# An FFT convolution with an expert layer on one core: whole-row loads, loads queued in another order, and an earlier hand-over to the experts

## The chip, the cores and the metric

The kernel runs on one core of a Trainium2 chip. TensorE (PE), VectorE (DVE), ScalarE (ACT) and GpSimd (POOL) compute; SyncE (SP) issues most DMAs, GpSimd issues the indirect ones. Each engine works through its own list of instructions in order. The metric is the time of one execution in microseconds (us), lower is better. The kernel before takes 2277.13 us, the median of three runs (2272.99, 2277.13 and 2289.8 us).

## The reference

```python
def _attn_ref(x, v, pos_emb, w1, w2):          # x, v: (4, 11456, 128)
    h_mlp = np.maximum(pos_emb @ w1, 0.0) @ w2
    h_filt = h_mlp * np.exp(-0.01 * pos)[:, None]
    u = x * v
    Uf = np.fft.rfft(u, n=2 * S, axis=1)
    Hf = np.fft.rfft(h_filt, n=2 * S, axis=0)
    y = np.fft.irfft(Uf * Hf[None], n=2 * S, axis=1)[:, :S, :]
    return x * y

def _moe_ref(x, modality_id, w_gate, modality_bias, w1, w2):   # x: (45824, 128), 8 experts
    logits = x @ w_gate + modality_bias[modality_id]
    e_idx = np.argmax(logits, axis=1)                          # one expert for each row
    gate_w = softmax(logits)[np.arange(N), e_idx]
    for e in range(E):
        mask = e_idx == e
        out[mask] = gate_w[mask, None] * (np.maximum(x[mask] @ w1[e], 0.0) @ w2[e])
```

Four sequences of 11,456 rows are convolved with one long filter; each resulting row then goes to one of eight experts (128 to 1024 to 128).

## The kernel before

**Stages.** Everything is written out in Python loops; a small class, `Timeline`, sorts the pieces by a time step, a place within the step and a rank, and so sets the order in which each engine's instructions are written. The filter comes first. Then, for each sequence b, an outer stage of 16 steps and a middle stage of 23 groups alternate. The outer stage of b does two things at once: it transforms sequence b forward, and it transforms sequence b-1 back and chooses the experts of its rows. So outer stage 0 has forward work alone, outer stages 1 to 3 have both, and a last outer stage (4) has the back half alone. The middle stage works on spectra. Then come the experts: tiles of 512 rows of one expert each, eight steps a tile (`experts`, L961), 99 tiles in all.

**One step of an outer stage.** The table `OUTER` (L57) gives each kind of work its delay in steps: `turn0:0` means that step t does this for q = t, `half:2` that it does it for q = t-2. In DVE's order a step holds: `product` (x times v, then a sum and a difference, L457 to L461), `choice` in every other step (the expert of each row, L758 to L779), `inverse` (L686 to L688, which ends in the multiplication with x into the buffer `xo`) and `send` in every other step (L804 to L811, the rows' places). In PE's order: turns (L672), `half` (L729, transposes of `xo`), `forward` (L472, reads what `product` wrote), `inverse` (L681), `logits`. The kinds in `LATE` (load, load_x, store, places) come at the end of a step; their DMAs are all in SP's one queue.

**The loads.** `load` (L446) brings x and v of block q as a tile of 128 partitions by 4 KB each into a ring of six buffers, three blocks deep. The sequences fill partitions 0 to 44 and 64 to 108; the rest of such a tile is padding. The first three blocks of a stage are read whole, to fill the buffers; later ones in two DMAs of 45 rows. `load_x` (the `load` at L662) brings another layout of x for `inverse` into a ring of four that it shares with the results y. The load of block q overwrites buffers of block q-3, which `forward` of q-3 reads on PE.

**Rows to the experts.** `store` (L784) writes rows of `xo` (three buffers) with their weight and number to DRAM (`xr`), `places` (L813) their target places (`xi`). When a sequence is done, `fetch` reads the places, and `rows_back` (L243) reads the rows, five blocks of 128 at a time, into one of three buffers; `send_rows` (L255) scatters one block of 128 rows per indirect DMA (L263) to its expert's region of `xs`. There are 90 blocks for each sequence. They are handed out in small numbers behind DVE instructions of the next stages (`paced`), at most eight under way at a time. `rows_back` for the next five is called with the first block of the present five, and waits until the buffer's former five are scattered.

**The hand-over.** A table of expert tiles (`first_table`) is computed from the counts known so far: `first` = 60 tiles that are surely full after three of four sequences. DVE computes it during the last outer stage. The load of a tile's rows (`rows_in`, L977) waits for the scatters that its table rests on. The last block of choices of sequence 3 (choice and store, then send and places) is left to the expert steps 8 and 14 (`FA`, `FB`), and its 90 scatters to later ones, with a second and a third table (`rest`).

Of the kernel before, what the change touches and what calls it, by code (L numbers as in the profile page):

```python
# [12 lines left out]
F32 = mybir.dt.float32  # L13
# [34 lines left out]
def surely_full(n):  # L48
# [7 lines left out]
NOWHERE = 1 << 20  # L56
OUTER = ("turn0:0 turn1:0 lturn:3 biased:3 half:2 product:-1 forward:1 choice:3 "  # L57
         "inverse:0 logits:2 send:4 load:-2 load_x:-2 store:4 places:5")
LAST = ("inverse:1 logits:3 turn0:0 half:2 lturn:3 turn1:0 biased:4 choice:4 load_x:-1 store:4 "
# [8 lines left out]
UNSURE = 5  # L68
FA, FB, FC = 8, 14, 18
NDYN = 8  # L70
# [106 lines left out]
def hyena_moe_kernel(ctx: ExitStack, tc: tile.TileContext, a: dict, out: bass.AP,  # L177
# [77 lines left out]
    def send_rows(n, behind=None, wait=None):  # L255


        for _ in range(min(n, len(waiting))):
            b, c = waiting.pop(0)
            if c % RC == 0:  # L260
                rows_back(b, c // RC + 1)
            ix, src = to_t[b % 2][:, c:c + 1], back_t[(b * NB + c // RC) % 3][:, c % RC]
            s = pool.indirect_dma_start(  # L263
                out=xs, out_offset=bass.IndirectOffsetOnAxis(ap=ix, axis=0), in_=src,
                in_offset=None, bounds_check=E * R - 1, oob_is_err=False)
            free_rows(scatters, s)
            if behind is not None:
                tc.add_manual_dep(ins_of(s), behind.name, order_dep, reason="order of issue")
            if wait is not None:
                tc.add_manual_dep(ins_of(s), wait.name, sync_dep, reason="pace")  # L270


    first = surely_full((nb - 1) * S) if nb > 1 else 0
    NW1 = min(nt, first)
# [79 lines left out]
    with ExitStack() as cv:  # L354
# [88 lines left out]
        def forward_stages(b):  # L443
            kept = {}

            def load(q):  # L446
                if q == 0:
                    from_first("seq")
                for name in ("xd", "v"):
                    t = kept[q, name] = ring("seq")  # L450
                    for p in (slice(0, HALF), slice(64, PU)) if q > 2 else (slice(0, D),):
                        sp.dma_start(t[p], a[name][b, q, p])

            def product(q):

                u, e = kept.pop((q, "xd"))[0:PU], kept.pop((q, "v"))[0:PU]
                paced(dve.tensor_mul(u, u, e))  # L457
                e = kept[q, "e"] = e.rearrange("p (c m) -> p c m", c=2)
                u = u.rearrange("p (w m) -> p w m", w=2)
                dve.tensor_add(e[:, 0], u[:, 0], u[:, 1])  # L460
                paced(dve.tensor_sub(e[:, 1], u[:, 0], u[:, 1]))  # L461

            def transform(q):

                e = kept.pop((q, "e")).rearrange("p c (j n) -> p c j n", n=N2)
                for h in range(2):
                    p = pair("s1")
                    for j in range(4):
                        for c in range(2):
                            for blk in range(2):  # L470
                                at = slice(64 * blk, 64 * blk + HALF)
                                pe.matmul(p[64 * c:64 * c + 64, blk, N1 * j:N1 * j + N1],  # L472
                                          e[at, c, 4 * h + j], fwd[at, c], start=True, stop=True)
# [351 lines left out]

        def before_last(f):
            return lambda q: f(q) if q < NQ - 1 else None

        def outer(b, at):
# [15 lines left out]
            if b == nb:  # L845
                for name in ("choice", "send", "store", "places"):
                    todo[name] = before_last(todo[name])
                finale.extend([lambda: (choice(NO - 1), store(NO - 1)),
                               lambda: (send(NO - 1), places(NO - 1))])
            def when(name, i, d):  # L850
# [24 lines left out]
        for b in range(nb + 1):  # L875
            outer(b, at)
            if b < nb:
# [5 lines left out]
                for k in range(3):  # L883
                    line.put(at - 1, lambda k=k: bias_of(k), 4, k)
            if b == nb - 1:
                line.put(at - 3, lambda: (dve.tensor_copy(base1, base),
                                          known.append((nb - 1) * NR // D)), 3)
        if NW1:
            gen = first_table(place)
            line.put(at - 1, lambda: [next(gen, 0) for _ in range(6)], 2)  # L890
            for k in range(NQ + 3):
                line.put(at + k, lambda: next(gen, 0), 3)
            line.put(at + NQ + 3, lambda: [0 for _ in gen], 4)
        else:
# [3 lines left out]
        line.run()  # L898
        send_rows(len(waiting))

# [13 lines left out]
    def rest():  # L914


        sp.dma_start(pad, a["c_pad"].rearrange("p (j r) -> p j r", j=TH // D))
        sp.dma_start(xs[E * R:E * R + TH, :].rearrange("(p j) r -> p j r", j=TH // D), pad)
# [42 lines left out]
    def experts(lo, hi):  # L961
# [116 lines left out]
        def rows_out(i):  # L1078
# [5 lines left out]
            for j in range(n // D):  # L1084
                pe.transpose(pt[:, D * j:D * j + D], k["oT"][:, D * j:D * j + D], ident)
            ot = mt.tile([D, 4, D], F32, tag="ot", name="ot", bufs=8)
            dve.tensor_mul(ot[:, 0:n // D], pt[:, 0:n].rearrange("p (j d) -> p j d", d=D),  # L1087
# [12 lines left out]
        for at in range(len(work) + 6):  # L1100
# [4 lines left out]
            if at < 2:  # L1105
                weights(lo, 2 + at)
            if lo == 0 and at in (FA, FB):
                finale[at == FB]()
            if lo == 0 and at == FC:
                fetch(nb - 1)  # L1110
            if lo == 0 and 4 * at % 15 < 4:
                send_rows(1)
            if NW1 - 14 <= i < NW1:
                next(others, 0)
# [57 lines left out]
```

## Time and profile before

| | |
|---|---|
| median of three runs | 2277.13 us |
| profiled execution | 2273.27 us |
| its span, first to last instruction | 2271.3 us |
| mean granted TensorE clock in it | 0.959 |
| PE busy | 2083.2 us (92%) |
| DVE busy | 1774.8 us (78%) |
| ACT busy | 1324.6 us (58%) |
| POOL busy | 1025.3 us (45%) |
| bytes moved by DMA | 343.10 MB |

The profile is of one execution. A busy share over the whole span mixes stages that are limited by different things, so it has to be cut into stages first: the filter up to about 100 us, outer stages from about 100, 283, 536, 795 and 1049 us on, middle stages from 172, 430, 688 and 949 us on, the experts from 1175 us to 2256 us. PE's clock in the rows is the granted share of full speed; 0.50 is the lower of its two levels.

### The profile page before, as it was taken

How to read it: one execution, taken by the hardware profiler on the slowest of the kernel's cores; microseconds unless marked ns; L12 is line 12 of the kernel's file. 1: busy time of each engine (PE TensorE's matmuls, PEld its weight loads, DVE VectorE, ACT ScalarE, POOL GpSimd, SP SyncE). 2: the span in 40 equal slices, each digit the busy share in tenths (PEclk: the TensorE clock that was granted, in tenths of full speed). 3: DMA queues.
4: the chain of work that ended last, by engine and by line, in shares of the span. 5: the costliest groups of instructions: out<-in, count | busy, mean ns of one | idle time of the engine just before them, and what ended most of it. 6: DMA issues, size and time to landing. Idle time of an engine off the chain costs nothing. (4 is left out here: it accounts for less than half of the span.)

```text
span 2271.3 us, 47560 instructions
## 1 busy us (share of the span) xinstructions
PE 2083.2 (92%) x17370; PEld 1633.9 (72%) x17370; DVE 1774.8 (78%) x2790; ACT 1324.6 (58%) x2467; POOL 1025.3 (45%) x932
## 2 busy tenths in 40 slices
PE   9979899788887888889969999999999999999996
PEld 8866656565555655566548888888888888888896
DVE  2368988998769977898767777777777877777796
ACT  5644466445544465445546666666666666666675
POOL 0104400396546955487735545555543333333332
PEclk9959999999889989999979999999999999999998
DMA  3886667677877778785768322222212111111110
GB/s 117 325 209 223 227 182 205 220 264 249 236 222 246 258 224 246 216 283 176 214 191 270 117 64 65 78 70 70 70 52 71 48 46 45 42 47 48 36 42 29
DMA packets 191990, 343.10 MB, mean 151 GB/s; under 512 B 33825, under 2 KB 101517, under 8 KB 191753
## 3 DMA queue, kind: packets, MB, share of 16 engines
q1 hardware_dynamic: 165097, 280.63, 40.6%
q0 software_dynamic: 26496, 59.36, 7.6%
q8 instruction: 139, 2.28, 0.4%
q14 instruction: 98, 0.80, 0.1%
q10 hardware_dynamic: 160, 0.03, 0.0%
HBM read 255.48 MB, written 84.83 MB: 150 GB/s over the span
## 5 line engine op out<-in xcount | busy, mean ns | idle before, releaser
L1054 DVE SCALAR_TENSOR_TENSOR hl<-ph,hh 128x512 fp32r<-128x512 f32 x724 | 498.8, 689 | 227.1 <-ACT hh L1053 217.6
L1053 ACT ACTIVATE hh<-ph 128x512 fp32r<-128x512 f32 x724 | 434.2, 600 | 361.7 <-PE ph L1050 357.3
L1090 POOL DMA_INDIRECT out<-ot,idx x362 | 357.3, 987 | 617.8 <-DVE ot L1087 511.6
L263 POOL DMA_INDIRECT xs<-back,to x360 | 433.0, 1203 | 210.5 <-issue 71.4
L1048 PE MATMUL ph<-xh,wh 128*128 128x512 f32 (+1 forms) x792 | 304.0, 384 | 2.0 <-ACT wh L1019 2.0
L1071 PE MATMUL po<-hh,wh 128*128 128x512 f32 (+1 forms) x792 | 303.4, 383 | 0.0
L1073 PE MATMUL po<-hl,wh 128*128 128x512 f32 (+1 forms) x792 | 295.3, 373 | 0.0
L1050 PE MATMUL ph<-xl,wh 128*128 128x512 f32 (+1 forms) x792 | 295.2, 373 | 0.0
L1049 PE MATMUL ph<-xh,wl 128*128 128x512 f32 (+1 forms) x792 | 294.1, 371 | 0.0
L1072 PE MATMUL po<-hh,wl 128*128 128x512 f32 (+1 forms) x792 | 294.0, 371 | 0.0
L649 PE MATMUL pw<-work 64*128 64x128 f32 x2880 | 205.8, 284 | 38.4 <-POOL work L637 31.2
L649 PEld LDWEIGHTS pw<-work 64*128 64x128 f32 x2880 | 174.1, 187 | 86.9 <-POOL work L637 44.8
L653 ACT COPY A<-pw 128x512 f32<-128x512 f32 (+1 forms) x184 | 97.1, 580 | 210.7 <-PE pw L649 210.7
L624 POOL TENSOR_TENSOR work<-work 128x512 f32<-128x512 f32 (+1 forms) x92 | 115.7, 1258 | 217.1 <-DVE work L620 211.8
L630 DVE TENSOR_TENSOR work<-pz,work 128x2048 f32<-128x2048 f32 (+1 forms) x92 | 205.5, 2234 | 0.0
L614 PE MATMUL pz<-A,work 128*64 128x256 f32 x1440 | 182.7, 397 | 16.6 <-DMA work<-in_c_to 7.9
L1050 PEld LDWEIGHTS ph<-xl,wh 128*128 128x128 f32 x792 | 149.4, 189 | 27.1
L1073 PEld LDWEIGHTS po<-hl,wh 128*128 128x128 f32 x792 | 149.1, 188 | 27.2 <-DVE hl L1054 0.2
L1048 PEld LDWEIGHTS ph<-xh,wh 128*128 128x128 f32 x792 | 149.6, 189 | 25.7 <-ACT wh L1019 2.4
L1049 PEld LDWEIGHTS ph<-xh,wl 128*128 128x128 f32 x792 | 150.0, 189 | 24.4 <-DVE wl L1020 0.4
L1072 PEld LDWEIGHTS po<-hh,wl 128*128 128x128 f32 x792 | 149.6, 189 | 22.9
L1071 PEld LDWEIGHTS po<-hh,wh 128*128 128x128 f32 x792 | 149.3, 189 | 22.2
(172 smaller groups left out, 3644.2 us busy)
## 6 DMA issues: line engine op xcount, KB each, us to landing
work<-hs SPq DMA_DIRECT2D x88, 512.0 KB
work<-in_x SPq DMA_DIRECT2D x64, 512.0 KB
work<-in_c_to SPq DMA_DIRECT2D x111, 256.0 KB
xr<-xo SPq DMA_DIRECT2D x64, 365.6 KB
back<-xr SPq DMA_DIRECT2D x72, 325.0 KB
work<-in_c_back SPq DMA_DIRECT2D x88, 256.0 KB
x<-xs SPq DMA_DIRECT2D x82, 260.0 KB
work<-in_xd SPq DMA_DIRECT2D x104, 180.0 KB
```

The costliest lines, as they stand in the source:

```text
L263: s = pool.indirect_dma_start(out=xs, out_offset=bass.IndirectOffsetOnAxis(ap=ix, axis=0), in_=src, in_offset=None, bounds_check=E * R - 1 ...
L630: dve.tensor_mul(m0[:, 0:n * 8 * D].rearrange("p (t c b d) -> p t c b d", c=2, b=2, d=D), z.unsqueeze(2).broadcast_to([D, 2 * n, 2, 2, D]) ...
L649: pe.matmul(v[s][:, t, blk], k["p"][at, t, r, blk], k["c"][at, t, r], start=r == 0, stop=r == 1)
L1048: pe.matmul(p, k[0, "h"][:, f:f + D], k["xh"], start=True, stop=False)
L1049: pe.matmul(p, k[0, "l"][:, f:f + D], k["xh"], start=False, stop=False)
L1050: pe.matmul(p, k[0, "h"][:, f:f + D], k["xl"], start=False, stop=True)
L1053: act.activation(hh, ph, AF.Relu)
L1054: dve.scalar_tensor_tensor(hl, ph, 0.0, hh.bitcast(F32), op0=ALU.max, op1=ALU.subtract)
L1071: pe.matmul(po, k[1, "h"][:, f], hh[:, t], start=g == 0, stop=False)
L1072: pe.matmul(po, k[1, "l"][:, f], hh[:, t], start=False, stop=False)
L1073: pe.matmul(po, k[1, "h"][:, f], hl[:, t], start=False, stop=g == NCH - 1)
L1090: s = pool.indirect_dma_start(out=out, out_offset=bass.IndirectOffsetOnAxis(ap=k["idx"][:, j:j + 1], axis=0), in_=ot[:, j, :], in_offset=N ...
```

## The change

Six things are done. The loads of x and v read all 128 partitions of a tile in one DMA in every block, and the product and forward transform use all of them. In `OUTER`, `product` is done one step later (0 in place of -1), `load_x` is issued one step later (-1 in place of -2) and stands ahead of `load` in the step. `rows_back` is called with the third block of five in place of the first. The first table of tiles rests on two sequences in place of three (37 tiles in place of 60) and is computed in fewer, fuller steps. The last two blocks of stores, sends and places, not the last one alone, are left to expert steps (2, 5, 8, 13 and 16). The scatters of sequence 3 come in five of nine expert steps in place of four of fifteen, and what was flushed ahead of the experts is not. One buffer of `ot` goes, of eight.

```diff
-OUTER = ("turn0:0 turn1:0 lturn:3 biased:3 half:2 product:-1 forward:1 choice:3 "
-         "inverse:0 logits:2 send:4 load:-2 load_x:-2 store:4 places:5")
+OUTER = ("turn0:0 turn1:0 lturn:3 biased:3 half:2 product:0 forward:1 choice:3 "
+         "inverse:0 logits:2 send:4 load_x:-1 load:-2 store:4 places:5")
...
-FA, FB, FC = 8, 14, 18
+FINALE, FC = (2, 5, 8, 13, 16), 18
+FR = 9
...
-            if c % RC == 0:
+            if c % RC == 2:
                 rows_back(b, c // RC + 1)
...
-    first = surely_full((nb - 1) * S) if nb > 1 else 0
+    NK = max(nb - 2, 0)
+    first = surely_full(NK * S) if NK else 0
...
-                    for p in (slice(0, HALF), slice(64, PU)) if q > 2 else (slice(0, D),):
-                        sp.dma_start(t[p], a[name][b, q, p])
+                    sp.dma_start(t, a[name][b, q])
...
-                u, e = kept.pop((q, "xd"))[0:PU], kept.pop((q, "v"))[0:PU]
+                u, e = kept.pop((q, "xd")), kept.pop((q, "v"))
...
-                                at = slice(64 * blk, 64 * blk + HALF)
+                                at = slice(64 * blk, 64 * blk + 64)
...
-                for name in ("choice", "send", "store", "places"):
-                    todo[name] = before_last(todo[name])
-                finale.extend([lambda: (choice(NO - 1), store(NO - 1)),
-                               lambda: (send(NO - 1), places(NO - 1))])
+                todo["choice"] = but_last(todo["choice"], 1)
+                for name in ("send", "store", "places"):
+                    todo[name] = but_last(todo[name], 2)
+                finale.extend([lambda: (store(NO - 2), send(NO - 2)), lambda: places(NO - 2),
+                               lambda: choice(NO - 1), lambda: (store(NO - 1), send(NO - 1)),
+                               lambda: places(NO - 1)])
...
-            if b == nb - 1:
+            if b == NK:
                 line.put(at - 3, lambda: (dve.tensor_copy(base1, base),
-                                          known.append((nb - 1) * NR // D)), 3)
+                                          known.append(NK * NR // D)), 3)
...
-        send_rows(len(waiting))
...
-            ot = mt.tile([D, 4, D], F32, tag="ot", name="ot", bufs=8)
+            ot = mt.tile([D, 4, D], F32, tag="ot", name="ot", bufs=7)
...
-            if lo == 0 and at in (FA, FB):
-                finale[at == FB]()
+            if lo == 0 and at in FINALE:
+                finale[FINALE.index(at)]()
...
-            if lo == 0 and 4 * at % 15 < 4:
+            if lo == 0 and 5 * at % 9 < 5:
                 send_rows(1)
-            if NW1 - 14 <= i < NW1:
+            if NW1 - FR <= i < NW1:
                 next(others, 0)
```

Two pieces of the order of instructions follow. Lines of the changed kernel are numbered up to three higher (L452 is L453, L666 is L667, L977 is L980).

SP's queue in outer stage 2, two steps of it, before (`in_xd` and `in_v` are x and v of `load`, `in_x` is `load_x`, `back<-xr` is `rows_back`, `xr<-xo` is `store`, `xi<-ix` is `places`):

```order
L247 DMA back_91<-xr_58 128x650
L452 DMA work<-in_xd 45x1024 x2
L452 DMA work<-in_v 45x1024 x2
L666 DMA work<-in_x 128x1024
L817 DMA xi_63<-ix_87 90x1x8 x2
L247 DMA back_92<-xr_58 128x650
L452 DMA work<-in_xd 45x1024 x2
L452 DMA work<-in_v 45x1024 x2
L666 DMA work<-in_x 128x1024
L788 DMA xr_59<-xo_83 90x1x1040 x2
```

and in the changed kernel:

```order
L248 DMA back_90<-xr_58 128x650
L667 DMA work<-in_x 128x1024
L453 DMA work<-in_xd 128x1024
L453 DMA work<-in_v 128x1024
L818 DMA xi_63<-ix_87 90x1x8 x2
L248 DMA back_91<-xr_58 128x650
L667 DMA work<-in_x 128x1024
L453 DMA work<-in_xd 128x1024
L453 DMA work<-in_v 128x1024
L789 DMA xr_59<-xo_83 90x1x1040 x2
```

`in_x` now stands ahead of the loads of x and v and of the stores, and belongs to the step after; `in_xd` and `in_v` are one DMA each. Beside the same DMAs DVE's `product` is one step later: the instructions of a step keep their places, and the block that is multiplied there is the one before.

The end of SP's queue ahead of the first expert tile, before (`x<-xs` is `rows_in`, `TENSOR_LOAD` and `ISA` read its address):

```order
L788 DMA xr_61<-xo_84 90x1x1040 x2
L666 DMA work<-in_x 128x1024
L817 DMA xi_65<-ix_86 90x1x8 x2
L788 DMA xr_61<-xo_85 90x1x1040 x2
L817 DMA xi_65<-ix_87 90x1x8 x2
L788 DMA xr_61<-xo_83 90x1x1040 x2
L817 DMA xi_65<-ix_86 90x1x8 x2
L974 TENSOR_LOAD tab_98
L977 ISA
L977 DMA x<-xs 128x520
```

and in the changed kernel:

```order
L789 DMA xr_61<-xo_84 90x1x1040 x2
L667 DMA work<-in_x 128x1024
L818 DMA xi_65<-ix_86 90x1x8 x2
L789 DMA xr_61<-xo_85 90x1x1040 x2
L818 DMA xi_65<-ix_87 90x1x8 x2
L977 TENSOR_LOAD tab_98
L980 ISA
L980 DMA x<-xs 128x520
```

The store and the places of the last block but one have left the queue ahead of the first tile's rows; they stand behind the loads of the third tile and of its weights. On PE the three small matmuls of that block's `send` have likewise moved from ahead of the first expert matmul to behind the third step's.

## Rows read from the trace of the kernel before

**Rows 1.** The page's second part: the span in 40 equal slices of 56.8 us, busy share in tenths; PEclk is the granted clock in tenths.

```profile
PE   9979899788887888889969999999999999999996
PEclk9959999999889989999979999999999999999998
```

**Rows 2.** Busy time of each engine (us, with the number of instructions) by stage: start and end of the stretch, its length, PE, PE's weight loads, DVE, ACT, POOL, then granted clock, busy share of the DMA engines, GB/s. In order: the middle of outer stage 0 (eleven steps); middle stage 0; the last outer stage; the gap ahead of the experts; the first expert tiles, and the rest of them.

```profile
121.60:163.20 41.60, 33.33 (x672) 28.33 (x676) 27.70 (x34) 15.17 (x20) 0.00 (x0) 0.53 0.95 208
172.00:283.00 111.00, 97.38 (x1080) 73.08 (x1080) 105.32 (x73) 50.97 (x93) 54.66 (x44) 0.97 0.66 222
...
1049.00:1148.00 99.00, 91.70 (x615) 59.58 (x615) 69.00 (x159) 59.80 (x122) 71.24 (x67) 1.00 0.67 206
1148.00:1175.00 27.00, 9.74 (x51) 5.82 (x43) 13.60 (x44) 5.20 (x12) 8.37 (x7) 0.62 0.53 142
1175.00:1260.00 85.00, 84.04 (x388) 68.64 (x389) 68.21 (x124) 54.67 (x101) 32.35 (x32) 0.98 0.83 264
1260.00:2256.00 996.00, 993.71 (x5088) 840.07 (x5086) 781.25 (x1359) 658.69 (x1216) 414.48 (x420) 1.00 0.18 56
```

**Rows 3.** The same view for stretches of whole pairs of steps, from one `inverse` on DVE (L686) to another: eight steps of outer stage 1, of 2 and of 3, then four early steps of the last outer stage and six late ones.

```profile
317.60:384.30 66.70, 59.74 (x828) 39.22 (x828) 56.97 (x118) 42.85 (x81) 0.00 (x0) 0.95 0.68 197
582.70:660.20 77.50, 64.09 (x840) 41.75 (x840) 56.86 (x117) 44.20 (x83) 41.19 (x36) 0.91 0.87 241
848.90:924.70 75.80, 64.74 (x836) 42.41 (x835) 56.85 (x117) 43.94 (x82) 41.51 (x36) 0.89 0.86 246
1066.50:1089.40 22.90, 22.90 (x158) 15.18 (x157) 15.15 (x34) 15.62 (x31) 17.68 (x18) 1.00 0.57 186
1104.70:1143.20 38.50, 34.51 (x227) 22.08 (x227) 28.70 (x76) 21.65 (x46) 30.27 (x28) 1.00 0.73 215
```

**Rows 4.** The waits of DVE (who waited, for what: us in total, times, longest), asked stage by stage: `product` for the load of v in 285 to 425 us, 545 to 685 us and 805 to 945 us, and `inverse` for the store of `xo` in 1052 to 1150 us.

```profile
DVE work L457 <- DMA work<-in_v: 9.6, 7, 2.6
DVE work L457 <- DMA work<-in_v: 22.1, 10, 4.3
DVE work L457 <- DMA work<-in_v: 20.9, 9, 3.7
DVE xo L688 <- DMA xr<-xo: 12.2, 4, 4.0
```

**Rows 5.** The waits of SP's queue, the same columns: `load_x` behind `inverse` in 545 to 685 us, then `rows_back` behind the scatters in 545 to 685 us and in 1052 to 1150 us.

```profile
SPq L666 <- DVE xo L688: 15.3, 6, 3.8
SPq L247 <- DMA xs<-back,to: 11.6, 8, 2.7
SPq L247 <- DMA xs<-back,to: 58.4, 20, 9.9
```

**Rows 6.** One step of outer stage 2 in order of time (start us, length us, engine, line, what; in brackets how long the engine had been idle and for what): from SP's queue a load of v, from DVE the end of a step (`inverse`) and the `product` that uses the load.

```profile
600.93 0.80 SPq L452 DMA_DIRECT2D work<-in_v  x2
603.14 1.23 DVE L688 TENSOR_TENSOR xo<-work 128x1024 f32<-128x1024 f32 x1
608.64 1.23 DVE L457 TENSOR_TENSOR work<-work 109x1024 f32<-109x1024 f32 x1 [4.27 <-DMA work<-in_v]
```

**Rows 7.** What DMA moved in 84 to 104 us: the summary line, and the transfers issued there, among them the first whole loads.

```profile
DMA packets 2329, 7.25 MB, mean 363 GB/s; under 512 B 255, under 2 KB 255, under 8 KB 2325
...
hs<-work POOLq DMA_DIRECT2D x6, 512.0 KB
...
work<-in_xd SPq DMA_DIRECT2D x3, 512.0 KB
work<-in_v SPq DMA_DIRECT2D x3, 512.0 KB
```

**Rows 8.** The hand-over in order of time, engine by engine (columns as in rows 6): DVE's late `inverse`; PE's last transposes of the choice and its first of the experts; SP's last stores and places and the first loads of expert rows.

```profile
1150.12 1.23 DVE L688 TENSOR_TENSOR xo<-work 128x1024 f32<-128x1024 f32 x1 [5.49 <-DMA xr<-xo]
1162.18 0.69 PE L744 MATMUL lt<-ident,work 128*109 128x128 f32 x4 [0.61 <-ACT work L739]
1171.81 1.09 PE L1031 MATMUL px<-ident,x 128*128 128x128 f32 x4 [8.81 <-DMA x<-xs]
1158.72 2.03 SPq L817 DMA_DIRECT2D xi<-ix  x2
1164.39 3.20 SPq L817 DMA_DIRECT2D xi<-ix  x2
1169.00 0.37 SPq L977 DMA_DIRECT2D x<-xs  x1
```

**Rows 9.** Groups of instructions by line (count, then busy us and mean ns of one, then idle time ahead): in 285 to 425 us DVE's multiplications over 128 and over 109 partitions; in the whole span PE's weight loads of 45 rows by 64 and of 128 rows by 64.

```profile
L688 DVE TENSOR_TENSOR xo<-work 128x1024 f32<-128x1024 f32 x16 | 19.6, 1227 | 0.5
L457 DVE TENSOR_TENSOR work<-work 109x1024 f32<-109x1024 f32 x15 | 18.3, 1221 | 9.6 <-DMA work<-in_v 9.6
...
L472 PEld LDWEIGHTS s<-fwd,work 45*64 45x64 f32 x4096 | 108.2, 158 | 51.3 <-ACT A L475 22.9 <-issue 11.1 <-DVE work L687 6.7
...
L614 PEld LDWEIGHTS pz<-A,work 128*64 128x64 f32 x1440 | 105.4, 141 | 65.8 <-issue 17.1 <-PE pw L649 9.1 <-PE pz L614 1.3
```

**Rows 10.** POOL in the expert steps in order of time (columns as in rows 6): the first scatters of two successive tiles' results (L1090), and one scatter of rows to the experts (L263) with the next.

```profile
1301.43 0.98 POOL L1090 DMA_INDIRECT out<-ot,idx  x1 [4.44 <-DVE ot L1087]
...
1306.56 0.98 POOL L263 DMA_INDIRECT xs<-back,to  x1 [0.31 <-issue]
1307.85 0.98 POOL L263 DMA_INDIRECT xs<-back,to  x1 [0.30 <-issue]
1313.24 0.98 POOL L1090 DMA_INDIRECT out<-ot,idx  x1 [4.41 <-DVE ot L1087]
```

More of the change, by code (lines that the diff above doesn't have):

```diff
@@ L824, in every_other, with but_last @@
             return lambda q: f(q // 2) if q % 2 == 1 else None
-        def before_last(f):
-            return lambda q: f(q) if q < NQ - 1 else None
+        def but_last(f, n):
+            return lambda q: f(q) if q < NQ - 2 * n else None
         def outer(b, at):
@@ L890, in hyena_moe_kernel @@
             line.put(at - 1, lambda: [next(gen, 0) for _ in range(6)], 2)
-            for k in range(NQ + 3):
-                line.put(at + k, lambda: next(gen, 0), 3)
-            line.put(at + NQ + 3, lambda: [0 for _ in gen], 4)
+            for k in range(NQ - 4):
+                line.put(at + k, lambda: (next(gen, 0), next(gen, 0)), 3)
+            line.put(at + NQ - 4, lambda: [0 for _ in gen], 4)
         else:
@@ L914, in rest @@
     def rest():
+        assert not waiting
         sp.dma_start(pad, a["c_pad"].rearrange("p (j r) -> p j r", j=TH // D))
```

## The prediction

> **What bounds the kernel now.** I read the slices first [rows 1]: PE is nearly full from the 23rd slice on and ragged before, so the experts are PE's and the outer and middle stages are not. Then the stages [rows 2]: in the experts PE is busy 993.71 of 996 us at full clock, so nothing done by another engine there can bring time, and nothing costs any that stays hidden. Middle stage 0 has DVE busy 105.32 of 111 us; the change leaves its work alone, and the later middle stages have the same. What is left are the outer stages and the gap of 27 us ahead of the experts, in which PE is busy for 9.74 us at a clock of 0.62.
>
> Within the outer stages I cut out eight equal steps each [rows 3]. Stages 1, 2 and 3 do the same DVE work there, 57 us, and take 66.7, 77.5 and 75.8 us: 8.34, 9.69 and 9.48 us a step. No engine is full: PE has 59.7 to 64.7 us (more at the lower clock), DVE 57. What differs is the DMA share, 0.68 against 0.87 and 0.86, since stages 2 and 3 also scatter a sequence. The waits [rows 4] say who pays: `product` waits for v 22.1 and 20.9 us in stages 2 and 3 and 9.6 us in stage 1. One step shows how [rows 6]: v is issued at 600.93, after the step's forward transform has freed its buffer, and `product` runs at 608.64 after 4.27 us of idling. The load takes some 7 us to land and gets one step of lead, whatever its size. A DVE that idles there is late with `inverse`, which follows, and so frees PE's result banks and the buffer of `load_x` late.
>
> **Product one step later.** DVE's work is the same; the load gets about one step more, 8 to 9 us, against waits of at most 4.3 us [rows 4], so I let this wait go. The forward transform follows `product` by one step in place of two; it comes after a `choice` and an `inverse` on DVE, so I price its wait at nothing; if DVE lags PE by a whole step the same 1 to 3 us a step come back there (second rival). `load_x` ahead of the loads no longer holds the stores behind `inverse` (15.3 us in stage 2 [rows 5]); it has a step less, but its buffer is free long before, so SP issues it without waiting.
>
> How much of the waits is time? From below: nothing, if PE or DMA takes the wait over. From above: PE's own pace, 5.73 us a step in the early last stage, where PE is busy for all 22.90 us [rows 3], plus the forward transform; 7.47 us of PE work a step in stage 1 is the nearest row for both, so at most 2.2 and 2.0 us a step in stages 2 and 3 and 0.9 in stage 1. I take 8.0 us a step for stage 1 and 8.6 for stages 2 and 3: a little over the present stage 1, which still has 9.6 us of the wait and no scatters. That is 0.34, 1.09 and 0.88 us a step. With 12 of 16 steps in the steady state: **-4, -13 and -11 us**, of which I take 2 off stage 2 for the state of its start: -4, -11, -11. Ends: 0 to -10, 0 to -26, 0 to -24.
>
> **Whole rows.** Each step's two loads grow from 4 x 184 KB = 737 KB to 2 x 524 KB = 1049 KB, and from four DMAs to two. The halved form alone moves 208 GB/s at a DMA share of 0.95, or 219 GB/s of busy time [rows 2]; whole rows move 222 at 0.66 (336) in middle stage 0, 264 at 0.83 (318) in the first experts [rows 2], and 363 GB/s where the first whole loads run [rows 7]. So a step's loads take 3.37 us of DMA before and 2.9 to 3.3 after: more bytes, no more time. The Trainium skill, page "DMA: Bandwidth & Descriptors", section "Anatomy of one DMA — SWDGE (gpsimd) path", speaks against it: a fixed time and then the bytes at 436 GB/s, which would add an estimated 0.7 us a step and turn the next term into +9. Its page "SBUF — State Buffer", section "Door 1: The DMA port swizzle", sides with the rows: a copy into the first 64 partitions reaches half the ports, 196 against 328 GB/s at 1 MiB, an estimated 3.8 us before and 3.2 after. The 208 GB/s agree with the second.
>
> Outer stage 0 is where this shows alone: 41.6 us for eleven steps, 3.78 us each, DMA full, PE busy for 3.03 us a step at a clock of 0.53 [rows 2]. With 2.9 to 3.3 us of DMA and PE's 3.03 I expect 3.3 to 3.4 us, 0.4 less in 13 steps: **-5 us**. Ends: +19 (first slower rival) and -10 (PE at full clock). The product over 128 partitions takes no longer (1227 against 1221 ns), nor does a weight load of 64 or more rows (141 for 128 rows, 158 for 45) [rows 9].
>
> **Last outer stage.** It moves no x and v of `load`. Early steps take 5.73 us with PE full, late ones 6.42 us [rows 3]; `inverse` waits 12.2 us for stores of `xo` [rows 4], and once more 5.49 us at the end [rows 8]. The stores are late because SP stands 58.4 us, 20 times 2.9 us, behind scatters for `rows_back` [rows 5]. Asked for two blocks later, two more scatters of about 1.3 us [rows 10] are done, so most of these 2.9 us go, and in stages 2 and 3 the 11.6 us. POOL itself gets no faster. PE idles 7.3 us of the 99 [rows 2] and some 5 us behind it; I take half: **-6 us**, ends 0 and -12.
>
> **Hand-over.** PE's last work of the stage starts at 1162.18 and its first transpose of expert rows at 1171.81, after 8.81 us of idling for the rows. Their load is issued at 1169.00, behind the stores and places of the last block but one, and serves PE 2.81 us later [rows 8]. With these moved behind it, it follows the places of 1158.72, which end at 1160.75; with the same 1.41 us from the last places' end (1167.59) to the issue it goes out at 1162.2, PE starts at 1165.0, 6.8 us earlier: **-7 us**. Ends: 0 (the tile's buffer or table holds it) and -9 (the clock, 0.62 there, falls less). The wait for three sequences' scatters goes too, but cost nothing visible.
>
> **Moved into the experts at no price.** The five pieces are DVE work in stretches where DVE is busy 781 of 996 us and PE was not held by the one block that is already there [rows 2]. Without that cover they would cost the 4 to 5 us of one `choice` and `send`. Scatters: 4.4 in place of 2.1 per tile beside four of results. At 1.29 us each [rows 10] that is 10.9 us of POOL per tile of 11.8 (1301.43 to 1313.24): close to full, but the buffers of `ot`, seven now, hold it, and 90 of them end after some 20 tiles, before the second table's work starts. Tile count and order within an expert's region stay.
>
> **Sum.** -5 -4 -11 -11 -6 -7 = -44 us. The profiled execution took 2273.27 us; that gives 2229, and the median lies 3.9 us above it, so **2233 us**. The scatter of the runs (2273 to 2290) means that 1%, 22.8 us, is about the least that can be told from no change: below 2254.4 is faster, above 2299.9 slower.
>
> **Rivals.**
> - *More than that* (0.08): the steps come down to PE's 7.5 us, and the clock, 0.89 to 0.95 [rows 3], recovers as PE idles less. For it: stage 1 has PE at 90% already. Against: DMA in stage 2 is busy 0.87 of 9.69, 8.43 us a step; with 2.9 to 3.3 us in place of 3.37 that is 8.0 to 8.4, so 8.6 leaves little. -5 -10 -26 -24 -10 -8 = -83 gives 2194.
> - *The wait changes hands* (0.20): PE waits for its banks or `forward` for `product`, and a third of the gain of stages 1 to 3 stays. For it: PE is busy 83 to 90% there [rows 3]. -5 -1 -4 -4 -6 -7 = -27 gives 2250.
> - *The wait for v stays* (0.10): the change does not do what it says, because the load still waits for `forward` three blocks back and DMA holds it for two steps. For it: the DMA share of 0.87. Against: 4.3 us is the longest wait. Only -5 -6 -7 are left: 2259.
> - *Bytes decide, slower* (0.08): whole rows move no faster per byte than halved ones. At 219 GB/s a step's loads take 4.79 us in place of 3.37. Stage 0 is then bound at (3.59 + 1.42) / 0.95 = 5.3 us a step, +19. In stages 2 and 3 DMA work grows from 8.43 and 8.15 us a step to 9.85 and 9.57; at a share of 0.97 that takes 10.15 and 9.87 us: +6 and +5. With -13 from the rest, 2273 + 4 + 17 = 2294. It decides below 247 GB/s, where the loads take 4.25 us and DMA fills 97% of 9.6 us; the rows for whole tiles have 318 or more. The rule of the page "DMA: Bandwidth & Descriptors" in the Trainium skill, bytes alone, is its milder form.
>
> **How the numbers follow.** The forecast has 0.54 and holds 2214 to 2252. Faster: 0.54, 0.08 and 0.14 of the second rival, 0.76. Slower, with 2294 so near the bound: half of the last rival, 0.04. The rest, 0.20, is no change. The range from 2197 to 2266 takes in the forecast, the second and third rivals and the near part of the first.
>
> **What would show it.** `product`'s wait for v near nothing in stages 2 and 3, and their steps at 8.6 us; if the steps stay at 9.5 with that wait gone, look for the new wait on PE or `forward`. The middle of stage 0 at over 250 GB/s and under 3.6 us a step; if not, whole rows are no faster. SP's wait for scatters in the last stage under 20 us. The idle time before the experts' first transpose near 2 us. A PE still full in the experts to the end: if it waits there around the 35th tile, the second table came late, and if results wait for POOL, the denser scatters are to blame; either would make the prediction wrong from a side that I price at nothing.

## The result and the profile after

| | before | after |
|---|---|---|
| median | 2278.23 us (4 runs, 2272.99 to 2289.8) | 2201.3 us (4 runs, 2199.77 to 2203.26) |
| ratio, 95% interval | | 0.9656 (0.9618 to 0.9694) |
| span of the profiled execution | 2271.3 us | 2198.8 us |
| mean granted TensorE clock | 0.959 | 0.984 |
| bytes moved by DMA | 343.10 MB | 359.27 MB |

The change is 77 us faster; 44 were forecast. Medians are of all executions, ratios of the fast ones, without those over 1.5% above the fastest of the same kernel. 16 MB more are moved, and the time is shorter. The slices of the page, as in [rows 1], now of 55 us each:

```profile
PE   8968899898988898889799999999999999999996
PEclk9999999999999999999899999999999999999998
```

The holes in the clock of before are gone, but for the 20th slice, and PE is even from the 21st slice on; before it was so from the 22nd (the prediction read the 23rd). Where the 72.5 us of the spans come from shows when both traces are cut at the same instructions: `inverse` on DVE (first and last of each outer stage) and the first transpose of the experts on PE.

| | before, us | after, us | difference |
|---|---|---|---|
| start to first `inverse` of outer stage 1 | 290.3 | 283.2 | -7.1 |
| outer stage 1, first to last `inverse` | 116.2 | 104.7 | -11.5 |
| outer stage 2 | 131.4 | 107.4 | -24.0 |
| outer stage 3 | 130.3 | 105.1 | -25.1 |
| the three middle stages between | 389.0 | 386.8 | -2.2 |
| last outer stage | 97.6 | 99.0 | +1.4 |
| last `inverse` to first transpose | 17.05 | 10.7 | -6.4 |
| first transpose to the end | 1099.5 | 1101.9 | +2.4 |

The same stretches by busy time (columns as in [rows 2, 3]): the middle of outer stage 0 between the same times as before; eight steps of outer stages 1, 2 and 3; the last outer stage.

```profile
121.60:163.20 41.60, 25.73 (x824) 21.51 (x816) 30.56 (x37) 18.69 (x26) 0.00 (x0) 0.92 0.93 330
```

```profile
324.27:382.84 58.57, 55.94 (x832) 38.39 (x830) 56.24 (x118) 42.64 (x81) 0.00 (x0) 1.00 0.77 264
560.30:619.04 58.74, 55.98 (x832) 38.42 (x830) 56.41 (x119) 42.93 (x81) 42.12 (x36) 1.00 0.98 345
795.78:854.80 59.02, 56.31 (x835) 38.74 (x833) 56.52 (x119) 43.05 (x82) 42.59 (x36) 1.00 0.99 346
988.00:1087.00 99.00, 88.65 (x570) 57.72 (x568) 66.01 (x158) 56.99 (x117) 76.48 (x72) 0.95 0.64 197
```

The three stages take 7.32, 7.34 and 7.38 us a step, whether a sequence is scattered beside them or not. DVE is busy for 56.2 to 56.5 us of each 58.6 to 59.0, 96%: its own work, 57 us before too [rows 3], is nearly what a step now lasts. PE follows at 95%, with 56 us in place of 59.7 to 64.7, all at a clock of 1.00; which of the two would hold a step alone was not tried. DMA is at 0.98 and 0.99 in stages 2 and 3, at 345 GB/s where it moved 241 and 246.

DVE's waits in outer stages 1, 2 and 3 (283 to 388, 517 to 625 and 754 to 860 us), the heads of three answers:

```profile
DVE work L687 <- ACT work L685: 4.9, 4, 2.3
```

```profile
DVE work L687 <- ACT work L685: 6.5, 4, 3.9
DVE xo L689 <- DMA xr<-xo: 1.0, 1, 1.0
```

```profile
DVE work L687 <- ACT work L685: 5.1, 5, 2.3
```

`product` (now L458) waits for v in none of them, where it had 9.6, 22.1 and 20.9 us [rows 4]. SP and DVE in the last outer stage, beside [rows 4, 5]:

```profile
SPq L248 <- DMA xs<-back,to: 58.3, 20, 11.4
...
DVE xo L689 <- DMA xr<-xo: 17.7, 5, 6.6
```

Nothing improved there: the scatters hold SP for the same 58 us in 20 waits, and `inverse` waits for the stores as long as before, 17.7 us (the 12.2 of [rows 4] and the 5.49 of [rows 8], which lies outside their window). The hand-over in order of time, beside [rows 8]:

```profile
1090.12 1.73 SPq L818 DMA_DIRECT2D xi<-ix  x2
1093.31 0.69 PE L745 MATMUL lt<-ident,work 128*109 128x128 f32 x4 [0.61 <-ACT work L740]
1094.13 0.36 SPq L980 DMA_DIRECT2D x<-xs  x1
...
1096.88 1.09 PE L1034 MATMUL px<-ident,x 128*128 128x128 f32 x4 [2.88 <-DMA x<-xs]
```

The rows' load goes out 0.8 us after PE's last work of the stage has begun, and PE idles for 2.88 us in place of 8.81.

### The profile page after: what moved, and what is told of

Same layout as the page of the kernel before. It is cut to its first block, busy times and chain, and to the rows that moved or that the text cites. A ratio compares the mean times of both kernels' runs of the same rounds, so it can differ in the third digit from the quotient of the medians.

```text
span 2198.8 us, 47378 instructions
## 1 busy us (share of the span) xinstructions
PE 2036.6 (93%) x17370; PEld 1607.3 (73%) x17370; DVE 1774.6 (81%) x2790; ACT 1322.8 (60%) x2467; POOL 1024.7 (47%) x932
## 2 busy tenths in 40 slices
DMA packets 194485, 359.27 MB, mean 163 GB/s; under 512 B 32369, under 2 KB 100061, under 8 KB 194249
## 4 chain that ended last, share of the span: by engine, by line
issue 35%; DVE 23%; PE 18%; POOL 9%; DMA 4%; ACT 2%; SPq 1%; POOLq 0%; DVEq 0%; ACTq 0%
POOL out L1093 8%; DVE work L631 7%; DVE work L621 4%; PE py L682 2%; DVE work L458 2%; PE po L1076 2%; PE ph L1053 2%; PE ph L1051 2%; PE ph L1052 2%; PE po L1074 2%; PE po L1075 2%; PE pw L650 1%; DVE xo L689 1%; PE wt L673 1%; PE pz L615 1%
```

## The experiments

There are twelve runs, in three series (the expectations say "call"). The kernel before was timed again in each. The length of a stage is read from one profiled execution: the kernel before and two of the first series that have its code for outer stage 1 took 112.8 to 116.2 us there, so a few us of one stage say little by themselves. In the first series, one part of the change at a time is made in the kernel before, which took 2273.14 us there.

**The order alone**: the new `OUTER` line and nothing else.

```diff
-OUTER = ("turn0:0 turn1:0 lturn:3 biased:3 half:2 product:-1 forward:1 choice:3 "
-         "inverse:0 logits:2 send:4 load:-2 load_x:-2 store:4 places:5")
+OUTER = ("turn0:0 turn1:0 lturn:3 biased:3 half:2 product:0 forward:1 choice:3 "
+         "inverse:0 logits:2 send:4 load_x:-1 load:-2 store:4 places:5")
```

> The kernel before with the new OUTER line alone (product a step later, load_x a step later and ahead of load); loads in halves, everything else as before. Theory 'lead': product idled because its load had one step to land, so a second step is enough even for halved loads: wait for v in stages 2 and 3 under 3 us each (22.1 and 20.9 before), steps there at 7.4 to 8.0 us, in all 40 to 60 us faster. Rival 'rate': DMA is full with halved loads (share 0.87), so a shorter step only fills it: steps stay at 8.6 us or more, at most 25 us faster.

Measured: 2228.24 us, ratio 0.9802 (0.9769 to 0.9835). Eight steps of outer stages 1, 2 and 3:

```profile
338.74:397.38 58.64, 56.02 (x833) 38.44 (x831) 56.31 (x118) 42.78 (x82) 0.00 (x0) 1.00 0.78 224
574.79:641.29 66.50, 60.31 (x820) 39.44 (x818) 56.53 (x118) 42.04 (x79) 39.74 (x36) 0.92 0.93 271
817.84:882.59 64.75, 59.21 (x829) 39.06 (x828) 56.49 (x118) 42.78 (x81) 40.25 (x36) 0.95 0.97 283
```

No wait for v is left in any of them. Stage 1, without scatters, is already at the 7.33 us of the full change. Stages 2 and 3 stop at 8.31 and 8.09 us, where DMA is busy for 0.93 and 0.97 of the time; with whole rows added, in the full change, they take 7.34 and 7.38. So with the wait gone, the halved loads are what holds them. The total is in the theory's 40 to 60 us, the steps of stages 2 and 3 a little over its 8.0.

**Whole rows alone**:

```diff
-                    for p in (slice(0, HALF), slice(64, PU)) if q > 2 else (slice(0, D),):
-                        sp.dma_start(t[p], a[name][b, q, p])
+                    sp.dma_start(t, a[name][b, q])
...
-                                at = slice(64 * blk, 64 * blk + HALF)
+                                at = slice(64 * blk, 64 * blk + 64)
```

> The kernel before with whole-row loads, product and forward transform over all partitions alone. Theory 'lead': outer stage 0 gains 5 to 7 us as in the changed kernel (3.72 to 3.34 us a step), but the wait for v in stages 2 and 3 stays at 12 us or more each; in all 8 to 20 us faster. Rival 'rate': the load lands early enough by itself, wait under 5 us each, 40 us faster or more.

Measured: 2254.95 us, ratio 0.9918 (0.9892 to 0.9945). Outer stage 0 goes at 3.48 us a step. Outer stage 2, eight steps, and the head of DVE's waits in 545 to 700 us:

```profile
575.45:648.20 72.75, 60.06 (x829) 40.87 (x828) 56.99 (x118) 42.78 (x81) 42.63 (x36) 0.95 0.84 279
```

```profile
DVE work L456 <- DMA work<-in_v: 19.6, 9, 3.5
```

A load in half as many DMAs and at a higher rate still comes too late: the wait is 19.6 us against 22.1 [rows 4], and a step takes 9.09 us. DMA is not full, at 0.84. So the wait for v in stages 2 and 3 is a matter of when the load is issued much more than of its rate.

**The hand-over alone** (first table from two sequences, stores of two blocks in `finale`, scatters in five of nine expert steps):

> The hand-over alone: first table from two sequences, last two blocks' stores, sends and places among the experts, denser scatters of sequence 3, seven buffers of ot; OUTER, loads and rows_back as before. PE's idle time ahead of the first expert transpose falls from 8.8 us to about 3; in all 4 to 8 us faster, outer stages unchanged. If the table had also held the last stage: 12 us or more.

Measured: 2274.64 us, ratio 0.9986 (0.9962 to 1.001). The stretch from the last `inverse` to the first transpose falls from 17.05 to 11.65 us, the stretch from there to the end grows from 1099.5 to 1102.3. What is left, 2.6 us, agrees with the ratio and can't be told from nothing. PE's idle time ahead of the first transpose is 3.02 us, as expected; the 4 to 8 us in all were not reached, since the experts give back half of it.

**Rows read back later, alone**:

```diff
-            if c % RC == 0:
+            if c % RC == 2:
```

> The kernel before with rows_back called with the third block of five alone. Theory 'POOL sets it': the wait of SP for scatters in the last stage falls from 58 us to about 40 and moves elsewhere, time within 4 us of before. Rival 'SP holds the stores': inverse no longer waits for stores of xo (12.2 us before) and the last stage is 5 to 8 us shorter.

Measured: 2270.68 us, ratio 0.9997 (0.9978 to 1.0017). SP's waits in the last outer stage, head of the answer:

```profile
SPq L247 <- DMA xs<-back,to: 58.7, 17, 9.9
```

58.7 us against 58.4 [rows 5]: the fall to 40 us that the theory had did not come, and the time stayed within its 4 us. Nor did the rival's gain: `inverse` waits 19.0 us for stores of `xo`, against 17.7 over the whole stage before. Asked for two scatters later, the buffer is again two or three scatters away (58.7 us in 17 waits, scatters 1.29 us apart [rows 10]): POOL, not the place of the request, sets when it comes free.

The four parts alone give -45, -18, +1.5 and -2.5 us by their medians, of which the last two are within their intervals of nothing. Their sum of 64 falls short of 77, by no more than the intervals allow. Stages 2 and 3 say where the difference can lie: the order alone takes 1.4 us off a step in each, whole rows alone 0.6 and 0.3 us, both together 2.35 and 2.1. If that is more than chance, order and rows give more together because each takes away a part of what holds the other.

**The second series** undid one part of the full change at a time. There the kernel before took 2347.35 us, so only stretches can be compared with the runs above, and the changed kernel itself was not among them. Loads in halves again:

> The changed kernel with the loads in halves of 45 rows again (product and forward transform over 109 partitions). Theory 'two limits': with the lead given, DMA is the limit of stages 2 and 3 if loads are halved: steps of 8.1 to 8.3 us there as with the order alone, 7.33 in stage 1, 3.7 to 3.8 in stage 0; 22 to 30 us slower than the changed kernel. Rival 'lead only': steps stay at 7.35, only stage 0 loses, 5 to 8 us.

`product` at its old place:

```diff
-OUTER = ("turn0:0 turn1:0 lturn:3 biased:3 half:2 product:0 forward:1 choice:3 "
+OUTER = ("turn0:0 turn1:0 lturn:3 biased:3 half:2 product:-1 forward:1 choice:3 "
```

> The changed kernel with product in its old step (-1), load_x still ahead of load. Theory 'lead': the wait for v comes back (over 8 us in each of stages 2 and 3), steps of 8.3 us or more there; 20 to 40 us slower than the changed kernel. Rival 'SP order': the gain came from load_x no longer standing between loads and stores; then this loses under 8 us.

`load_x` at its old step and place (`load:-2 load_x:-2`):

> The changed kernel with load_x at its old step and behind load (-2). Theory 'lead': loads still have two steps; within 5 us of the changed kernel. Rival 'SP order': SP stands behind inverse again, stores and loads are late, 10 to 30 us slower.

Three scatters a step in the last outer stage, not five. This form reads the first rows of sequence 3 into a buffer that blocks of sequence 2 still need, so some blocks scatter other rows and the output is wrong; the number of scatters is the same.

```diff
-                paced(dve.tensor_add(y[:, 0:512], py[:, 0], y[:, 512:1024]), 2 * n - 1)
+                paced(dve.tensor_add(y[:, 0:512], py[:, 0], y[:, 512:1024]), 1)
```

> The changed kernel with 3 scatters in place of 5 a step in the last outer stage (24 blocks of sequence 2 are then scattered among the experts). Theory 'POOL sets the last stage': SP's wait for scatters falls from 42 us to under 10, inverse no longer waits 17.7 us for stores of xo, the stage goes from 99 to 90 us or less; 5 to 9 us faster, if the denser POOL among the experts costs nothing. Rival 'PE and the stores': the stage stays within 3 us.

| undone | median, us | ratio to before (interval) | us a step: outer 0, 1, 2, 3 | last stage, us |
|---|---|---|---|---|
| whole rows | 2357.82 | 1.0061 (1.0022 to 1.01) | 3.70, 7.33, 9.44, 9.16 | 128.5 |
| `product` later | 2351.88 | 1.0018 (0.9987 to 1.005) | 3.49, 8.13, 8.87, 9.16 | 136.7 |
| `load_x` later | 2337.38 | 0.996 (0.9931 to 0.9989) | 3.36, 7.33, 8.88, 9.30 | 141.0 |
| five scatters a step | 2299.9 | 0.9821 (0.9749 to 0.9892) | 3.28, 7.33, 10.23, 9.17 | 90.2 |

The totals did not come out as expected: outer stages with scatters are long in this series whatever is undone. Outer stages 0 and 1, which have none, answer: whole rows are worth 0.3 to 0.4 us a step in stage 0 (3.70 against 3.36 and 3.28) and, with the new order, nothing in stage 1; `product` is worth the 0.8 us of stage 1, where the wait for v is back:

```profile
DVE work L458 <- DMA work<-in_v: 12.0, 7, 2.7
```

`load_x` is worth nothing in either. What each is worth in stages 2 and 3 this series doesn't show.

**The third series** therefore has the changed kernel beside two of the undone ones and beside the version with three scatters, in which the rows of sequence 3 are now fetched later (`FC` 48 in place of 18), when no block of sequence 2 needs their buffer. The kernel before took 2368.85 us there.

> The changed kernel itself, as it is, beside the three that follow on the same chip: what is undone there is compared with this. On a chip on which the kernel before takes some 2275 us: 2201 us, steps of 7.3 us in outer stages 1 to 3, as in its first profile. On the chip of the last four runs, where the kernel before took 2347 us and only stages with scatters were long: if those stages are long there for the changed kernel too (theory: that chip's scatters are slower, not the change), steps of 7.3 in outer stage 1, over 8.5 in outer stages 2 and 3, and some 2330 to 2350 us in all. The rival, that the edits undone in the last four runs were what made the stages long: 7.3 in outer stages 2 and 3 and some 2270 us.

Measured: 2345.8 us, ratio 0.9894 (0.9832 to 0.9956), 23 us faster than before in place of 77. The rival falls: nothing is undone here, and outer stage 1 takes 7.33 us a step, stages 2 and 3 take 9.51 and 9.34, the last stage 140.6 us. That it is the chip, as the theory has it, is not shown: this series ran on a chip of the same number, 6, as the first, where the kernel before took 2273.14 us, and the second on number 4. Four stretches: eight steps of outer stages 1 and 2, the last outer stage, and 500 us of experts.

```profile
327.23:385.89 58.66, 55.96 (x832) 38.36 (x830) 56.32 (x118) 42.62 (x81) 0.00 (x0) 1.00 0.78 263
571.68:647.74 76.06, 63.79 (x830) 43.68 (x829) 57.72 (x119) 43.78 (x81) 41.56 (x37) 0.93 0.81 263
...
1043.00:1183.00 140.00, 107.93 (x559) 63.02 (x557) 66.66 (x157) 59.47 (x115) 75.38 (x72) 0.80 0.49 139
...
1400.00:1900.00 500.00, 487.87 (x2261) 397.77 (x2260) 372.60 (x658) 310.12 (x565) 193.99 (x196) 0.98 0.18 55
```

Stage 1 is the same as in the first profile to 0.1 us. In stage 2 DMA is at 0.81, where it was at 0.98, and no engine is full.

> The changed kernel with the halved loads of 45 rows back. Theory: with the lead in the order the bytes' pace decides: outer stage 0 at 3.7 to 3.8 us a step in place of 3.3 (-> +6 us), outer stage 1 still at 7.3, outer stages 2 and 3, where scatters and rows read back come on top, at 8.1 to 8.3 where the chip is the usual one (-> +8 us each from 8 steps of the steady part, more over 15), in all +20 to +30 us against the changed kernel of this call. The rival, that the lead alone does it and whole rows are worth only stage 0: +5 to +8 us.

Measured: 2370.64 us, 24.8 more than the changed kernel beside it; ratio to before 0.9983 (0.9946 to 1.002). Outer stage 0 takes 3.78 us a step against 3.43, stage 1 the same 7.33: these are as the theory has them, and so is the total, though the two intervals just overlap. Stages 2 and 3 are 5.6 and 10.0 us longer (139.8 and 137.2 us), which shows little: the last run of this series has the same code there as the changed kernel and takes 131.3 and 130.9 us in place of 134.2 and 127.2. The two profiled executions differ by 13 us, not 24.8.

> The changed kernel with the product one step earlier again (product:-1), whole rows kept. Theory: the lead of one step between the load's issue and the product is what ended the wait for v: the wait comes back at each product (5 to 12 us where rows are read back), outer stage 1 at 8.0 to 8.2 us a step in place of 7.3, outer stages 2 and 3 at 8.8 to 9.2, in all +30 to +50 us against the changed kernel of this call. The rival, that whole rows arrive soon enough without the lead: 7.3 to 7.5 a step and within 8 us.

Measured: 2358.81 us, 13.0 more, with intervals that overlap; ratio to before 0.9953 (0.9919 to 0.9988). Stage 1 is as expected, 8.23 us a step against 7.33, with the wait for v back:

```profile
DVE work L458 <- DMA work<-in_v: 8.9, 7, 2.7
```

Stages 2 and 3 are not: 129.4 and 130.3 us against 134.2 and 127.2. The 30 to 50 us did not come; in this series something else holds these stages.

> The changed kernel with 3 scatters a step in the last outer stage in place of 5 (those left over go out among the first experts' blocks, and the rows of the last sequence are fetched at block 48 in place of 18). Theory: in the last stage SP stands behind the scatters and the stores behind SP, so DVE waits for the output buffer: with fewer scatters a step that wait goes, the stage takes some 90 us in place of 99 and the kernel is 5 to 9 us faster than the changed one of this call. The rival, that the last stage is bounded by DVE as the others are (7.3 us a step): no change within 3 us. A second rival: what is taken out of the stage comes back in the experts, where POOL has more to do beside the tables: the stage is shorter and the experts longer by as much.

Measured: 2315.66 us, ratio 0.9704 (0.9645 to 0.9762): 30 us less than the changed kernel beside it, with intervals that do not meet, and so faster than both kernels in that series. The expected gain was 5 to 9 us. The last stage takes 90.3 us against 140.6; that stage and 500 us of the experts:

```profile
1044.00:1134.00 90.00, 87.32 (x576) 55.38 (x575) 65.38 (x155) 58.54 (x118) 43.70 (x45) 1.00 0.62 181
...
1353.00:1853.00 500.00, 477.97 (x2196) 387.50 (x2195) 360.73 (x639) 301.17 (x549) 209.75 (x212) 0.98 0.19 58
```

PE is nearly full in the last stage. SP's wait for scatters there, first in the changed kernel of this series, then in this version:

```profile
SPq L248 <- DMA xs<-back,to: 12.9, 2, 9.8
```

```profile
SPq L248 <- DMA xs<-back,to: 2.1, 3, 1.4
```

That is 11 us less of this wait in a stage that is 50 us shorter, so the theory's chain, from scatters over SP to the stores, is not what most of the gain comes from. Some of the gain comes back: from the first transpose to the end it takes 1175 us against 1151, half the second rival. What this version does where the changed kernel takes 2201 us was not tried; its last stage of 99 us there, against 90 here, makes about 9 us the most to expect of it (an estimate).

## Why the prediction was right in sign and short in size

**Product one step later: the mechanism held, the size was too small.** The wait for v went, as said, and came back when `product` alone was put back (8.13 and 8.23 us a step in stage 1, with 12.0 and 8.9 us of waits). The term that was mis-sized is the choice of 8.0 and 8.6 us a step. The steps came down to 7.32 to 7.38 us, below even the end of 7.47 us, so that these stages and the middle stages between gave 62.8 us in place of 26. That end was no bound: it was PE's busy time of a step at a clock of 0.95, and PE's busy time fell to 7.0 us. So stages 1 and 3, with -11.5 and -25.1, lie outside their ends of -10 and -24. This is the first rival, "more than that", with 0.08: its 2194 us lies nearer to 2201 than my 2233, and 2201 lies outside the forecast's own 2214 to 2252. The range down to 2197 holds it because the rival's near part was taken in, by 4 us.

What spoke against that rival was a busy share read as work: DMA 0.87 of 9.69 us, so at least 8.0 us a step. It was not a fixed amount. A step of stage 2 moved 241 GB/s x 9.69 us = 2.34 MB in 8.4 us of busy time before; after, it moves 345 x 7.34 = 2.53 MB in 7.2. More bytes took less of DMA's time. The rate while busy was 277 GB/s (241 / 0.87) before, 291 with the order alone (271 / 0.93), 332 with whole rows alone (279 / 0.84) and 352 with both (345 / 0.98). I had corrected the loads by rows of whole tiles and left the other 5 us of each step as they were. At least the scatters among them became shorter too: their queue's packets, MB and share of DMA's time in the eight steps of stage 2 (77.5 us before, 58.74 after), before and then after:

```profile
q0 software_dynamic: 1159, 2.40, 10.6%
```

```profile
q0 software_dynamic: 1103, 2.28, 10.5%
```

That is 1.03 us a step before and 0.77 after, for nearly the same bytes.

The clock, named in the same rival, moved too: 0.89 to 0.95 before [rows 3], 1.00 after. PE's busy time of a step of stage 2 fell from 8.0 us (64.09 / 8) to 7.0. How much of the step's time the clock itself had cost is not shown: in stage 1 whole rows alone had a clock of 1.00 at 7.93 us a step, so a step can be long without it.

```profile
328.56:392.00 63.44, 57.25 (x831) 38.38 (x829) 57.01 (x118) 42.45 (x81) 0.00 (x0) 1.00 0.75 247
```

**Whole rows: right in stage 0.** Twelve steps there went from 3.72 to 3.34 us, -4.7 against the forecast's -5; the start of stage 1 moved by -7.1. DMA moves 330 GB/s there in place of 208, over the 250 that were named as the mark, and 3.34 us a step lie in the 3.3 to 3.4 of the sum. The rival "bytes decide" fell with it. The Trainium skill's page "SBUF — State Buffer", section "Door 1: The DMA port swizzle", has 196 and 328 GB/s for a copy into the first 64 partitions and for one into all, and the 208 and 330 here lie near the two, though the halved form here is two copies, one into either half. The rule of its page "DMA: Bandwidth & Descriptors", section "Anatomy of one DMA — SWDGE (gpsimd) path", a fixed time and then the bytes, is given for DMAs that GpSimd issues, and SP issues these; read by the bytes alone, as the prediction did, it would have made the steps of stage 0 longer. They became shorter, so it does not serve to compare copies into a part of the partitions with copies into all. In stages 2 and 3 whole rows are worth more than in stage 0, which the sum did not have: with the order alone these stages took 115.0 and 110.9 us, with the full change 107.4 and 105.1.

**`load_x` ahead of the loads: costs and brings nothing in outer stages 0 and 1.** I said that SP would issue it without waiting. It waits for `inverse` as before, 36.7 us in 7 waits in stage 1 (29.5 before). DVE has no wait for it there, and putting it back left both stages as they were. What it does in stages 2 and 3 is not shown.

**Last outer stage: wrong.** -6 forecast, +1.4 measured. The step that failed is that two scatters later the ones that SP waits for are done: SP stood for 58 us in either place, in the full change and with this part alone. POOL is busy for 76.48 of 99 us there, so a request that comes later most likely meets a later scatter. SP's wait "under 20 us", my own mark for this step, was missed. In stage 2, where the same wait of 11.6 us was to go as well, it is 22.2 us (517 to 625 us), though DVE waits there only 1.0 us for the stores behind it. With three scatters a step the wait is 2.1 us, but in a series in which the changed kernel itself has only 12.9, so what that would bring here is open.

**Hand-over: right**, -7 forecast, -6.4 measured; 2.88 us of idling against about 2. The 2.4 us that the experts got longer come off this.

**The experts: nearly nothing, as priced.** +2.4 us, with PE busy for 996.20 of 998 us:

```profile
1185.00:2183.00 998.00, 996.20 (x5092) 840.64 (x5090) 784.36 (x1359) 659.50 (x1217) 408.99 (x412) 1.00 0.18 55
```

With the hand-over alone they were 2.8 us longer, with each of the other parts alone within 0.7 us of before, so it is this part that costs them; in what wait was not settled.

## What to carry to other kernels

Where a load has one step of lead and its user waits, ask first when it is issued: here a step more of lead ended the wait, and a higher rate alone left most of it (19.6 of 22.1 us in stage 2). Price a step then by the work of the engine that is left fullest (here DVE, with 7.0 of 7.3 us), not by a little below what it took. A transfer's rate matters where DMA is what then holds the stage, so two edits can be worth more together than one by one. A busy share of DMA, and busy time of PE at a lowered clock, are not fixed amounts of work: here the one fell from 8.4 to 7.2 us a step with more bytes, the other from 8.0 to 7.0.

## What the hardware showed that was not expected

The kernel before took 2278 us in the runs of the result and 2273 us in the first series, but 2347 and 2369 us in the other two, and the changed one 2201 us in the runs of the result and 2346 us in the third series. The number of the chip does not tell these apart, as said. The extra time lies in stretches in which POOL scatters, though not in all of them. Outer stage 1, without scatters, takes 7.33 us a step in every series with the new order; the last outer stage, with some 70, takes 99.0 and 140.6 us; the three middle stages, with 22 to 27 each, take 386.8 and 390.3 us together. In the long stretches PE and DVE stand idle in part for nothing that the profile shows ("issue"). PE's and DVE's waits in the last outer stage of the changed kernel in the third series:

```profile
PE wt L673 <- issue: 10.7, 6, 2.9
PE lt L745 <- issue: 7.6, 4, 3.6
```

```profile
DVE ro L805 <- PE pr L803: 31.2, 4, 9.8
DVE work L687 <- ACT work L685: 26.0, 8, 10.5
DVE work L687 <- issue: 7.5, 3, 4.4
```

In the first profile PE and DVE have no wait for "issue" there and none for `pr`, and the one for ACT is 11.5 us. In the experts it is the same: DVE's waits in 1400 to 1900 us of the third series, where the first profile has only waits for ACT of more than 0.2 us.

```profile
DVE hl L1057 <- ACT hh L1056: 82.0, 137, 4.5
DVE hl L1057 <- issue: 35.2, 48, 2.4
```

PE is busy there for 487.87 of 500 us, and for 500.00 in the same kind of stretch of the first profile. What holds the engines up was not settled. That it goes with the scatters, and with the loads by `rows_back` that belong to them, is shown by the version with three a step: its last outer stage has 27 scatters fewer (x45 against x72 in the rows of POOL) and is 50 us shorter, and its experts, to which these scatters moved, are 24 us longer.
